# Attention and gated FFN on one core: the normalizing products move from VectorE to GpSimd, and the planned order is made anew

## The chip, the cores and the metric

The kernel runs on one core of a Trainium2 chip. The time is the device time of one execution in microseconds (us); lower is better. The profile shows one execution of the program, engine by engine: PE is TensorE (PEld its weight loads), DVE is VectorE, ACT is ScalarE, POOL is GpSimd, SP is SyncE, which here only issues DMA transfers.

## What is computed

```python
def reference(A_x, A_wqkv, A_wo, B_x, B_w_gate, B_w_up, B_w_down, gate_w):
    # x: 2048 x 512, 32 heads of width 16, F = 1376; all bfloat16
    x = A_x
    g = sigmoid((x * gate_w).sum(-1, keepdims=True))
    q, k, v = heads(x @ A_wqkv)
    p = softmax(q @ k.T * 16 ** -0.5)            # per head, 2048 x 2048
    a = merge_heads(p @ v) @ A_wo
    b = ((x @ B_w_gate) * (x @ B_w_up)) @ B_w_down
    return g * a + (1 - g) * b
```

The softmax is computed without a maximum: a column of ones beside each head's v makes the matmul with v also give the sum of the exponentials, and the attention output is divided by that sum afterwards. This division is the "normalizing product" of the title.

## The kernel before

**Tiling.** The queries come in 4 chunks of 512, the heads in 4 groups of 8. One chunk and one group are a *block* (16 of them, `bi` 0 to 15, about 40 us each); a block has two *quads* of 4 heads. For each quad and each of the 16 key tiles TensorE makes four score tiles of 128x512 in PSUM (tiles `QM` by `KT`; lines L1825 and L1803), the exponentials of them are made, and TensorE multiplies them with v (`Vp`, or the scaled copies `Vs`) into the output bank of the quad. TensorE works as eight tiles of 64x32 in two row halves.

**Two ways for the exponential.** For 10 of 16 key tiles ScalarE makes it (L1922; one to three score tiles at a time). For most of the other six (`dks`) VectorE makes a cheap 16-bit integer approximation in a buffer `DB` (L1962, the "pass"), and three copies of that buffer with a small integer added (steps v = 1, 2, 3) are multiplied with the scaled `Vs`, which refines the approximation. A copy is one 64-bit integer addition on GpSimd (`int64_add`, L1969, whole or in halves) or, more seldom, one instruction on VectorE (L1968). The buffers are the 8 of `DB` and, later on, the storage of `wv` and `wk`, which is why copies also read `DB<-wv`, `wk<-DB` and so on.

**Fillers.** Projections of q, k and v and the gated FFN run as filler matmuls between the attention work; VectorE evacuates them.

**The normalizing chain of a block.** VectorE copies the two output banks to `oc` and `oraw` (L2030); small transfers bring the sums together (`den8`); VectorE takes reciprocals (`recip`, L2044); they go out to DRAM (`scr_w`, tile `rscr`) and come back spread over the partitions (`rbc`, tile `rb`); and `mult` (L2133) makes `OT = oc * rb`, which later goes through the output projection. `oc` may be overwritten by the next block's copy only after `mult`. For the last block (15) half of the heads are normalized by another way at the very end (`tail_norm`, `tail_out`).

**Who sets the order.** `_Sched` is a planner that runs when the kernel is built: an event loop with a price for each kind of instruction decides for each engine what comes next, by rules and by tables in `PAR` with one value per microsecond of planned time. What comes out is one fixed list of instructions per engine, with semaphore waits between them. At run time each engine goes through its list in that order and stops at an instruction whose inputs are late. Relevant parts are `try_pool` (what GpSimd does next; `ptask` is a list of tasks for it, empty in this version; `small` holds VectorE's small tasks, the product among them), `issue` and `try_sp`: TensorE's instructions come in blocks of 256, the planner counts them (`icount`, `inext`), and the transfers whose price is in `BULK` are issued only in a window of time that is set from each block crossing (`land`), to keep them away from the fetch of the next block. Where the planner puts a `BULK` transfer in a window, the transfer also waits for a TensorE instruction.

**GpSimd's preparation.** The prologue runs a dummy `int64_add` on a tiny tile `lib` (L2179 and L2180) long before the first copy. Ahead of it the compiled program holds a pair of MODIFY_POOL_CONFIG instructions which the source does not name. A second such pair stands ahead of the one TENSOR_TENSOR that GpSimd executes in this version, an addition in `tail_out` (L2107) at the very end.

Of the kernel before, what the change touches and what calls it, by code (L numbers as in the profile page):

```python
# [12 lines left out]
ALU = mybir.AluOpType  # L13
# [123 lines left out]
class _Sched:  # L137
# [117 lines left out]
    def issue(self, r, n, key=None):  # L255
# [83 lines left out]
    def s_a(self, r):  # L339
        i = self.apos[r]  # L340
        p = None
        if self.apend[r] is None:
# [478 lines left out]
    def pe_phase(self, r):  # L821
        if self.ends():
            return self.pe_end(r)
        if self.g("lw") and self.lw[r]:
# [311 lines left out]
    def try_pool(self):  # L1136
# [5 lines left out]
        for x in self.ptask:  # L1142
            if x[0] <= now:
                self.ptask.remove(x)
                self.log("pool", x[1], x[3])
                self.pool_v = self.lock_v = self.now + x[1]
                self.at(self.pool_v)
                x[2]()
                return True
# [5 lines left out]
        for e in self.cpq:  # L1155
# [10 lines left out]
            else:  # L1166
                return False
            if not self.cp_buf(e, v):
                return False
# [9 lines left out]
            return True  # L1179
        return False  # L1180
# [7 lines left out]
    BULK = (2.0, 3.4, 4.0, 4.2)  # L1188

    def try_sp(self):  # L1190
# [3 lines left out]
        free = now > self.par["spend"] or self.land - 0.85 <= now + 1e-9 <= self.land + 0.05  # L1194
# [156 lines left out]
    def norm2(self, bi):  # L1351
# [21 lines left out]
    def norm3(self, bi, o):  # L1373
        c, b = divmod(bi, 4)
        op = self.hw.mult(bi, [o] + self.dep([("x", ch) for ch in range(1, min(self.par["xq"], 2) + 1)]) + self.rdep(("ocb", bi)) + self.rdep(("outl", c - 2))) if self.hw else None
# [260 lines left out]
    def run(self):  # L1636
# [54 lines left out]
        self.fullm, self.fullend = False, 0.0  # L1691
        self.lw, self.lk = [None, None], [None, None]
# [41 lines left out]
class _Hw:  # L1734
# [397 lines left out]
    def mult(self, bi, deps):  # L2132
        return self.dve(lambda v: v.tensor_tensor(self.OT[:, bi % 8, :], self.oc[:], self.rb[:], ALU.mult), deps)  # L2133
# [18 lines left out]
    def prologue(self):  # L2152
# [112 lines left out]
        for var in (0, 1):  # L2265
# [23 lines left out]
 'alook': ((7, 6), (1, 5), (2, 2), (1, 4), (3, 2), (1, 6), (15, 2), (1, 4), (43, 2), (1, 3), (12, 2), (1, 3), (2, 6), (1, 2), (2, 6), (2, 2), (1, 6),  # L2289
# [541 lines left out]
```

## Time and profile before

| | |
|---|---|
| time, median of 3 runs | 656.09 us (654.62 to 781.75) |
| the profiled execution's own time | 655.02 us |
| its span in the profile | 652.9 us |
| PE busy | 646.0 us, 99% |
| ACT busy | 638.9 us, 98% |
| DVE busy | 603.7 us, 92% |
| POOL busy | 523.3 us, 80% |
| granted TensorE clock | 1.00 |

The span leaves out 2.1 us of the profiled execution's time, which lie around it. Busy times count an engine as busy while an instruction of it runs; a busy PE is not necessarily one that has all eight tiles at work. Register, branch, semaphore and DMA-issuing instructions are not counted as busy.

### The profile page before, as it was taken

Reading aid. Unit: us, or ns where it says so; the run is one execution under the profiler, and the core shown is the slowest. Engines: PE = TensorE matmul, PEld = TensorE weight load, DVE = VectorE, ACT = ScalarE, POOL = GpSimd, SP = SyncE. Lnnn points to the kernel's source line nnn. Section 1 sums busy time; section 2 is a strip of 40 time slices with the busy share of each in tenths; the row PEclk is TensorE's granted clock in tenths of the full one; section 3 lists DMA queues with packets and bytes.
Section 4 is the critical chain, followed back from the end, with each engine's and each line's share of the span. In section 5 each row is a group of like instructions: output and inputs, shape, how many; then the busy total and the mean of one; then the engine's idle time right before and its main releaser. Section 6 shows DMA issues by size and latency. Waiting matters only on the chain.

```text
span 652.9 us, 46802 instructions
## 1 busy us (share of the span) xinstructions
PE 646.0 (99%) x22683; PEld 374.7 (57%) x20716; DVE 603.7 (92%) x996; ACT 638.9 (98%) x776; POOL 523.3 (80%) x602
## 2 busy tenths in 40 slices
PE   9999999999999999999999999999999999999997
PEld 4666556555555565555555655555555566665664
DVE  7899999999998989999999989999998899998995
ACT  6999999999999999999999999999999999999996
POOL 4229887898898999898999677899898756977871
PEclk9999999999999999999999999999999999999999
DMA  9201222221210100101001010100101011010101
GB/s 176 67 5 44 61 55 66 32 50 54 77 41 20 32 28 21 31 5 31 12 20 32 13 47 21 32 13 13 31 7 42 19 30 34 5 31 21 30 6 50
DMA packets 32498, 22.89 MB, mean 35 GB/s; under 512 B 17356, under 2 KB 29036, under 8 KB 32304
## 3 DMA queue, kind: packets, MB, share of 16 engines
q1 hardware_dynamic: 30784, 18.86, 11.5%
q8 instruction: 169, 2.77, 1.8%
q10 hardware_dynamic: 1488, 1.05, 0.7%
q14 instruction: 25, 0.20, 0.1%
q0 software_dynamic: 32, 0.00, 0.0%
HBM read 12.23 MB, written 2.36 MB: 22 GB/s over the span
## 4 chain that ended last, share of the span: by engine, by line
PE 95%; DVE 2%; POOL 1%; DMA 1%; ACT 1%; issue 0%; POOLq 0%; ACTq 0%; DVEq 0%
PE ps L1825 86%; PE ps L1803 9%; DVE DB L1962 1%; DMA wq<-in_A_wqkv_dram 1%; POOL DB L1969 0%; ACT wu L1922 0%; PE ps L2243 0%; POOLq L87 0%; PE ps L2075 0%; DVE hT L2004 0%; POOL wk L1969 0%; POOL wq L2062 0%; ACTq L2159 0%; ACT oc L2103 0%; DVE wk L1968 0%
## 5 line engine op out<-in xcount | busy, mean ns | idle before, releaser
L1825 PE MATMUL ps<-QM,KT 64*32 64x512 bf16 x6224 | 462.5, 378 | 0.3 <-issue 0.2
L1969 POOL INT64_ADD DB<-DB x385 | 341.1, 901 | 84.0 <-DVE DB L1962 29.1
L1962 DVE TENSOR_SCALAR DB<-ps 128x512 int16<-128x512 f32 x576 | 378.0, 689 | 25.3 <-PE ps L1825 21.2
L1922 ACT ACTIVATE PT<-ps 128x1024 bf16<-128x1024 f32 (+1 forms) x349 | 301.4, 949 | 1.5 <-PE ps L1803 0.6
L1825 PE MATMUL ps<-DB,Vs 64*17 64x512 bf16 x3368 | 300.8, 376 | 0.6 <-POOL DB L1969 0.4
L1922 ACT ACTIVATE xT<-ps 128x1024 bf16<-128x1024 f32 (+1 forms) x264 | 239.5, 987 | 0.7 <-PE ps L1825 0.6
L1825 PEld LDWEIGHTS ps<-QM,KT 64*32 64x32 bf16 x6224 | 140.4, 89 | 140.5 <-DVE DB L1962 32.1
L1803 PE MATMUL ps<-QM,KT 64*32 64x512 bf16 x1968 | 194.0, 376 | 0.1
L1825 PE MATMUL ps<-PT,Vp 64*17 64x512 bf16 x1222 | 170.4, 376 | 0.0
L1825 PE MATMUL ps<-xT,Vp 64*17 64x512 bf16 x960 | 143.6, 376 | 0.0
L1825 PE MATMUL ps<-DB,Vp 64*17 64x512 bf16 x1160 | 116.2, 376 | 0.0
L1825 PE MATMUL ps<-xT,wg 64*32 64x512 bf16 x1376 | 108.9, 376 | 0.0
L1825 PE MATMUL ps<-xT,wu 64*32 64x512 bf16 x1376 | 108.5, 377 | 0.0
L1825 PEld LDWEIGHTS ps<-DB,Vs 64*17 64x17 bf16 x3368 | 85.7, 86 | 28.3 <-PE ps L1825 3.8
L1825 PE MATMUL ps<-wd,hT 64*32 64x512 bf16 x1408 | 99.7, 376 | 0.0
L1922 ACT ACTIVATE wd<-ps 128x1024 bf16<-128x1024 f32 (+1 forms) x88 | 76.1, 955 | 0.5 <-PE ps L1803 0.2
L1969 POOL INT64_ADD wv<-DB x61 | 54.7, 901 | 3.0 <-DVE DB L1968 1.0
L1969 POOL INT64_ADD DB<-wk x51 | 43.6, 873 | 7.4 <-DVE wk L1962 4.9
L1825 PEld LDWEIGHTS ps<-PT,Vp 64*17 64x17 bf16 x1222 | 43.9, 86 | 9.9 <-PE ps L1825 2.3
L1825 PE MATMUL ps<-wv,Vs 64*17 64x512 bf16 x448 | 45.0, 376 | 0.0
L1825 PEld LDWEIGHTS ps<-xT,wg 64*32 64x32 bf16 x1376 | 36.8, 91 | 13.6 <-issue 2.3
L1969 POOL INT64_ADD DB<-wv x41 | 37.3, 924 | 8.9 <-DVE OT L2133 3.7
(126 smaller groups left out, 869.5 us busy)
## 6 DMA issues: line engine op xcount, KB each, us to landing
rb<-rscr SPq DMA_DIRECT2D x16, 256.0 KB
QM<-qraw SPq DMA_DIRECT2D x124, 16.0 KB, 2.3
oc<-oraw SPq DMA_DIRECT2D x60, 32.0 KB, 2.4
out_dram<-ost SPq DMA_DIRECT2D x12, 128.0 KB, 2.0
wd<-in_B_w_down_dram SPq DMA_DIRECT2D x10, 128.0 KB, 2.7
wu<-in_B_w_up_dram SPq DMA_DIRECT2D x12, 96.0 KB, 2.3
wg<-in_B_w_gate_dram SPq DMA_DIRECT2D x12, 96.0 KB, 2.6
OT<-in_A_x_dram SPq DMA_DIRECT2D x2, 256.0 KB, 3.5
```

Source lines behind the costliest of these rows:

```text
L1803: return pe.add_instruction(mybir.InstMatmult(name=self.nc.get_next_instruction_name(), engine=pe.engine, ins=[pe.lower_ap(rhs), pe.lower_ ...
L1825: o = pe.matmul(dst, lhs, rhs, start=st, stop=sp, tile_position=(64 * r, 32 * cc), skip_group_check=True)
L1922: return self.P.op("act", lambda a: a.activation(dst, src, ACT.Exp, scale=self.ES), deps)
L1962: return self.dve(lambda v: v.tensor_scalar(dst, src, self.YB, 0.0, ALU.add, ALU.max), deps)
L1969: return self.P.op("pool", lambda e: e.int64_add(o.bitcast(I64), a.bitcast(I64), 32 * v * 0x0001000100010001), deps)
```

## The change

Four things are changed in the planner, and one in the program it makes:

1. `mult` of blocks 0 to 14 becomes a GpSimd instruction; that of block 15 stays on VectorE. In the planner it becomes a `ptask` with a price of 1.29 us in place of a small VectorE task of 0.598 us. `try_pool` takes it when no copy can be started, or at once when it has been ready for `PLAG` = 6 us.
2. The window for `BULK` transfers moves: it ran from 0.87 to 1.77 us behind a block crossing and runs from 0 to 0.95 us behind it. The transfers of the reciprocals to DRAM (price 1.85) become `BULK`. A block is counted as 255.7 instructions.
3. The rule that takes PSUM banks in pairs for score tiles gets two more modes (`apair` 5 and 6), which may take a pair across the two row halves.
4. All 42 tables of `PAR` with values per microsecond have new values; no single-valued entry changes. So the order of the instructions is new on every engine.

```diff
-            self.inext += 256
+            self.inext += 255.7
             self.land = self.now + 1.72
...
-            self.at(self.land - 0.85)
...
-            if i % 2 == 0 and self.g("apair"):
-                p = self.pair_pick(self.g("apair") > 2) if self.nb["A"] + 2 <= self.g("amax") else None
-                if p is None and self.g("apair") in (2, 4):
+            if (i % 2 == 0 and self.g("apair")) or (self.g("apair") > 4 and self.apend[1 - r] is None):
+                p = self.pair_pick(2 < self.g("apair") < 5) if self.nb["A"] + 2 <= self.g("amax") else None
+                if p is None and self.g("apair") in (2, 4, 6):
                     return False
...
-            bank, self.apend[r] = self.take_pair("A", p)
+            o = 1 - r if self.g("apair") > 4 and self.apend[1 - r] is None else r
+            self.across[o] = o != r
+            bank, self.apend[o] = self.take_pair("A", p)
...
 def try_pool(self):
-        for x in self.ptask:
-            if x[0] <= now:
-                ...
-                return True
+        if self.pool_task(now - self.PLAG):
+            return True
...
-                return False
+                return self.pool_task(now)
...
+    PLAG = 6.0
+
+    def pool_task(self, now):
+        for x in self.ptask:
+            if x[0] <= now:
+                self.ptask.remove(x)
+                self.log("pool", x[1], x[3])
+                self.pool_v = self.lock_v = self.now + x[1]
+                self.at(self.pool_v)
+                x[2]()
+                return True
         return False
...
-    BULK = (2.0, 3.4, 4.0, 4.2)
+    BULK = (1.85, 2.0, 3.4, 4.0, 4.2)
...
-        free = now > self.par["spend"] or self.land - 0.85 <= now + 1e-9 <= self.land + 0.05
+        free = now > self.par["spend"] or self.land - 1.72 <= now + 1e-9 <= self.land - 0.77
...
-                    self.small.append((t2 + self.par["mmarg"], 0.598, lambda: self.norm3(bi, o2), ("M", bi)))
+                    if bi < 15:
+                        self.ptask.append((t2 + self.par["mmarg"], 1.29, lambda: self.norm3(bi, o2), ("M", bi)))
+                        self.at(t2 + self.par["mmarg"] + self.PLAG)
+                    else:
+                        self.small.append((t2 + self.par["mmarg"], 0.598, lambda: self.norm3(bi, o2), ("M", bi)))
...
     def mult(self, bi, deps):
-        return self.dve(lambda v: v.tensor_tensor(self.OT[:, bi % 8, :], self.oc[:], self.rb[:], ALU.mult), deps)
+        return self.P.op("pool" if bi < 15 else "dve", lambda v: v.tensor_tensor(self.OT[:, bi % 8, :], self.oc[:], self.rb[:], ALU.mult), deps)
...
  PAR = {
- 'alook': ((7, 6), (1, 5), (2, 2), (1, 4), (3, 2), (1, 6), (15, 2), (1, 4), (43, 2), ...
+ 'alook': ((8, 6), (5, 2), (2, 5), (67, 2), (1, 3), (5, 2), (1, 6), (12, 2), (1, 6), ...
```

How the lists move is shown at three places. The rows are the compiled lists of one engine, in order: line, operation, output tile and input tiles, shape, how often in a row, and the semaphores waited for (`s_pe0`, `s_pe1`, `s_dve`, `s_pool`: those engines; `s_drb`, `s_docb`, `s_dscr`: the transfers into `rb`, into `oc` and to `rscr`). A row ISA with two tiles is a copy; a bare row ISA is a pair of MODIFY_POOL_CONFIG. Lines of the changed kernel are 20 to 30 higher.

GpSimd before, the copies that it made while VectorE made the first product (at 78 us):

```order
L1969 ISA DB<-DB 128x1024 [waits s_pe1]
L1969 ISA wv<-DB 128x1024 [waits s_pe0]
L1969 ISA DB<-DB 128x1024 [waits s_pool,s_dve]
L1969 ISA DB<-DB 128x1024 [waits s_dve,s_pe0]
L1969 ISA DB<-DB 128x1024 [waits s_pool]
L1969 ISA DB<-DB 128x1024 [waits s_pe1]
```

GpSimd after, around the first product:

```order
L1993 ISA DB<-DB 128x1024 [waits s_pool,s_dve]
L1993 ISA wv<-DB 128x1024 [waits s_pe0]
L1993 ISA DB<-DB 128x1024 [waits s_pe1]
L2157 ISA
L2157 TENSOR_TENSOR OT<-oc,rb 128x512 [waits s_drb,s_docb]
L1993 ISA
L1993 ISA DB<-DB 128x1024 [waits s_dve,s_pe0]
L1993 ISA DB<-DB 128x1024 [waits s_pe1]
L1993 ISA DB<-DB 128x512 [waits s_pe0]
L1993 ISA DB<-DB 128x512
```

Between two copies there now stand a bare ISA, the product, and another bare ISA. The same three rows stand at each of the 15 products: the list of GpSimd has 3 bare ISA before and 33 after.

VectorE before, around the first product and the copy of the next block's output into `oc`:

```order
L1962 TENSOR_SCALAR DB<-ps 128x512 [waits s_pe0]
L1968 TENSOR_SCALAR DB<-DB 128x2048
L2133 TENSOR_TENSOR OT<-oc,rb 128x512 [waits s_drb,s_docb]
L1962 TENSOR_SCALAR DB<-ps 128x512 [waits s_pe1]
L2030 TENSOR_TENSOR oc<-ps,erow 128x512 [waits s_dve,s_pe0]
L2004 TENSOR_TENSOR hT<-ps,usb 128x512 [waits s_pe1]
```

VectorE after, around the same copy:

```order
L1986 TENSOR_SCALAR DB<-ps 128x512 [waits s_pe0] x2
L1986 TENSOR_SCALAR DB<-ps 128x512 [waits s_pe1]
L1986 TENSOR_SCALAR DB<-ps 128x512 [waits s_pe0]
L2054 TENSOR_TENSOR oc<-ps,erow 128x512 [waits s_pool]
L1986 TENSOR_SCALAR DB<-ps 128x512 [waits s_pe1]
L2028 TENSOR_TENSOR hT<-ps,usb 128x512 [waits s_pe0]
```

The product is gone from VectorE's list, and the copy into `oc` waits for GpSimd instead.

SyncE before, the transfers of the second block's reciprocals:

```order
L2040 DMA oc<-oraw 16x512 x3
L2130 DMA rscr<-rec 4x16x32 [waits s_dve]
L2130 DMA rscr<-rec 4x16x32
L2056 DMA wg<-in_B_w_gate_dram 128x384 [waits s_pe0]
L2125 DMA rb<-rscr 128x1x512 [waits s_dscr,s_pe1]
```

SyncE after:

```order
L2064 DMA oc<-oraw 16x512 x3
L2080 DMA wu<-in_B_w_up_dram 128x384 [waits s_pe0]
L2154 DMA rscr<-rec 4x16x32 [waits s_pe0] x2
L2149 DMA rb<-rscr 128x1x512 [waits s_dscr,s_pe0]
L2080 DMA wu<-in_B_w_up_dram 128x384 [waits s_pe1]
```

The transfers to `rscr` now wait for TensorE too, that is for a window behind a block crossing.

The amount of work stays as it is: 22687 matmuls before and 22679 after, 1352 score tiles exponentiated by ScalarE in 763 instructions before and 767 after, 696 score tiles passed by VectorE in both, 369 transfers and other rows of SyncE in both. GpSimd's copies are 394 whole ones and 194 halves before, 379 and 227 after.

More of the change, by code (lines that the diff above doesn't have):

```diff
@@ L823, in pe_phase @@
             return self.pe_end(r)
+        if self.across[r]:
+            if self.apend[r] is None:
+                self.across[r] = False
+            elif self.s_a(r):
+                return True
         if self.g("lw") and self.lw[r]:
@@ L1141, in try_pool @@
         now = self.now + 1e-9
-        for x in self.ptask:
-            if x[0] <= now:
[L1144 to L1148, printed above, removed]
-                return True
+        if self.pool_task(now - self.PLAG):
+            return True
         if self.dve4_until + 0.063 > now:
@@ L1166, in try_pool @@
             else:
-                return False
+                return self.pool_task(now)
             if not self.cp_buf(e, v):
-                return False
+                return self.pool_task(now)
             for k in hs:
@@ L1179, in try_pool @@
             return True
+        return self.pool_task(now)
+    PLAG = 6.0
[7 more added lines that the diff above has]
+                x[2]()
+                return True
         return False
@@ L1374, in norm3 @@
         c, b = divmod(bi, 4)
-        op = self.hw.mult(bi, [o] + self.dep([("x", ch) for ch in range(1, min(self.par["xq"], 2) + 1)]) + self.rdep(("ocb", bi)) + self.rdep(("outl", c - 2))) if self.hw else None
+        op = None
+        if self.hw:
+            deps = [o] + self.dep([("x", ch) for ch in range(1, min(self.par["xq"], 2) + 1)]) + self.rdep(("ocb", bi)) + self.rdep(("outl", c - 2))
+            op = self.hw.mult(bi, deps + ([self.last4] if bi < 15 else []))
+        if bi < 15:
+            self.setr(("ot", bi), self.now + 1.29 + 0.044 + 0.05, op)
+            return
         self.last4 = op
@@ L1691, in run @@
         self.fullm, self.fullend = False, 0.0
+        self.across = [False, False]
         self.lw, self.lk = [None, None], [None, None]
@@ new lines @@
+ 'anyb': 0,
+ 'apair': ((7, 0), (1, 3), (4, 2), (1, 1), (2, 0), (1, 1), (3, 0), (1, 3), (7, 0), (1, 4), (2, 0), (1, 1), (4, 0), (2, 1), (1, 3), (3, 1), (1, 0),
[15 rows of a table added]
+ 'apick': ((8, 0), (35, 1), (5, 0), (2, 1), (2, 0), (4, 1), (13, 0), (2, 1), (3, 0), (1, 1), (1, 0), (6, 1), (1, 0), (5, 1), (1, 0), (12, 1), (1, 0),
[8 rows of a table added]
+ 'ares': ((12, 2), (1, 1), (2, 2), (1, 1), (5, 2), (10, 1), (4, 2), (2, 1), (1, 2), (4, 1), (4, 2), (2, 3), (2, 2), (2, 3), (1, 1), (3, 2), (8, 3),
[10 rows of a table added]
+ 'await': ((7, 0.6), (1, 0.05), (3, 0.6), (1, 0.05), (4, 0.1), (5, 0.05), (2, 0.1), (1, 0), (4, 0.1), (1, 0.05), (1, 0.22), (1, 0.45), (4, 0),
[17 rows of a table added]
@@ new lines @@
+ 'cpmax': ((8, 20), (5, 5), (3, 20), (5, 5), (4, 8), (1, 3), (5, 8), (4, 10), (8, 8), (3, 30), (1, 14), (1, 5), (2, 10), (2, 14), (1, 10), (11, 14),
[13 rows of a table added]
+ 'dact': ((26, 2), (1, 5), (25, 2), (1, 5), (15, 2), (3, 5), (2, 2), (9, 5), (1, 2), (3, 5), (2, 3), (1, 2), (3, 3), (5, 5), (1, 2), (2, 4), (1, 5),
[11 rows of a table added]
+ 'dahead': ((8, 0), (5, 1), (3, 2), (5, 1), (4, 0), (1, 1), (3, 0), (1, 1), (3, 0), (2, 1), (11, 0), (2, 1), (2, 0), (2, 1), (4, 2), (3, 1), (6, 0),
[9 rows of a table added]
+ 'dend': ((7, 2), (1, 4), (7, 2), (1, 0), (15, 2), (1, 0), (3, 5), (8, 2), (3, 0), (2, 1), (1, 0), (1, 4), (2, 1), (1, 2), (16, 1), (2, 4), (3, 1),
[11 rows of a table added]
@@ new lines @@
+ 'dresv': ((16, 1), (4, 0), (1, 1), (1, 0), (1, 1), (5, 0), (2, 1), (1, 0), (4, 1), (13, 0), (2, 1), (1, 0), (1, 1), (12, 0), (1, 1), (37, 0), (3, 1),
[7 rows of a table added]
+ 'dwait': ((6, 0), (1, 0.1), (1, 0.4), (3, 0), (1, 0.6), (1, 0.2), (3, 0), (5, 0.6), (7, 0), (1, 0.6), (1, 0.4), (1, 0.1), (4, 0.6), (11, 0.1),
[16 rows of a table added]
+ 'fcf': ((22, 1), (1, 0), (7, 1), (1, 0), (15, 1), (2, 0), (2, 1), (2, 0), (1, 1), (33, 0), (2, 1), (1, 0), (3, 1), (2, 0), (3, 1), (6, 0), (2, 1),
+        (20, 0), (1, 1), (1, 0), (1, 1), (83, 0), (2, 1), (9, 0), (2, 1), (73, 0), (1, 1), (51, 0), (4, 1), (48, 0), (1, 1), (4, 0), (2, 1),
+        (93, 0), (4, 1), (1, 0), (2, 1), (4, 0), (2, 1), (34, 0), (1, 1), (8, 0), (2, 1), (2, 0), (1, 1), (4, 0), (1, 1), (17, 0), (1, 1), (10, 0),
+        (1, 1), (50, 0)),
@@ new lines @@
+ 'flim': ((42, 99), (1, 0), (80, 99), (3, 8), (2, 99), (1, 4), (34, 99), (1, 2), (1, 0), (2, 99), (4, 2), (19, 99), (5, 4), (20, 99), (1, 8),
[4 rows of a table added]
+ 'fmax': ((6, 3), (1, 1), (12, 3), (1, 2), (2, 3), (1, 2), (23, 3), (2, 2), (1, 1), (1, 3), (2, 2), (1, 3), (20, 2), (1, 1), (14, 2), (1, 3), (3, 2),
[9 rows of a table added]
+ 'fres': ((8, 1), (79, 0), (1, 1), (45, 0), (1, 1), (11, 0), (1, 1), (5, 0), (1, 1), (62, 0), (1, 1), (1, 0), (1, 1), (14, 0), (8, 1), (3, 0),
[10 rows of a table added]
+ 'fstart': ((21, 2), (25, 1), (2, 2), (2, 1), (2, 2), (1, 1), (39, 2), (6, 1), (4, 2), (3, 1), (1, 2), (6, 1), (16, 2), (1, 1), (11, 2), (2, 1),
[6 rows of a table added]
@@ L2648 @@
+ 'ghalf': ((13, 0.1), (2, 0.5), (1, 0.7), (1, 0.1), (3, 0.5), (1, 0.1), (8, -1), (1, 0.3), (1, -1), (4, 0.7), (8, -1), (3, 0.7), (2, 0.3), (1, 0.5),
[15 rows of a table added]
+ 'gwin': ((15, 0.2), (1, 0), (5, 0.2), (6, 0.8), (1, 1.2), (1, 0.8), (1, 0.2), (8, 0.8), (4, 0.2), (4, 0.8), (2, 1.2), (2, 0.8), (2, 0.5), (1, 0.8),
[15 rows of a table added]
  'ift': 3.55,
```

54 lines of the change are left out of this document (16 added, 38 removed), and 852 rows, old and new, of the table PAR.

## The prediction

> **What bounds the kernel now.** I read the busy times first, then the chain that ended last, then what PE waited for:
>
> ```profile
> span 652.9 us, 46802 instructions
> PE 646.0 (99%) x22683; PEld 374.7 (57%) x20716; DVE 603.7 (92%) x996; ACT 638.9 (98%) x776; POOL 523.3 (80%) x602
> ...
> PE 95%; DVE 2%; POOL 1%; DMA 1%; ACT 1%; issue 0%; POOLq 0%; ACTq 0%; DVEq 0%
> ...
> PE ps L1825 <- POOL DB L1969: 0.4, 1, 0.4
> ```
>
> PE runs 646.0 of 652.9 us, ACT 638.9, and 95% of the chain is PE. The longest wait of a matmul for a copy of POOL was 0.4 us. So the planned order fits the machine almost without a gap, and there is next to no idle time on PE or ACT from which a new delay could be paid: a delay that reaches PE goes into the total. Since the amount of matmuls, exponentials and passes stays the same (22687 and 22679 matmuls, 1352 score tiles for ACT, 696 for DVE), the change can win at most what PE now stands idle, 6.9 us, part of it at the start and the end. What it can lose has no such limit.
>
> POOL, which gets the new work, is the engine with the most room, but that room is in small pieces:
>
> ```profile
> core 0: us, PE busy (x) PEld busy (x) DVE busy (x) ACT busy (x) POOL busy (x), PEclk, DMA share, GB/s
> 0.00:24.00 24.00, 22.60 (x528) 13.00 (x472) 19.30 (x48) 18.28 (x32) 8.50 (x16) 1.00 0.81 164
> ...
> 200.00:300.00 100.00, 99.82 (x3564) 55.63 (x3232) 92.63 (x148) 99.30 (x125) 94.10 (x112) 1.00 0.08 22
> ```
>
> ```profile
> L1969 POOL INT64_ADD DB<-DB x385: 603/1037/1060, 13.8 to 636.6; - x193
> ...
>   DVE DB L1962: 30.8, 27
>   PE ps L1825: 28.1, 21
>   DVE DB L1968: 19.1, 9
>   PE ps L1803: 9.3, 7
> ...
>   PEld ps L1825: 3.1, 9
> ```
>
> A whole copy takes 1.04 us, a half 0.61. Ahead of copies POOL was idle for 87.3 us in these 64 waits, 1.4 us each on average. The last row is the other side: weight loads waited for copies 9 times, 3.1 us in all, so copies come just in time. How early they come is seen where a tile can be told apart by its name, at the first copies into `wv` and into `wk` and the first matmuls that read them:
>
> ```profile
> 50.65 1.04 POOL L1969 INT64_ADD wv<-DB  x1
> ...
> 53.83 0.39 PE L1825 MATMUL ps<-wv,Vs 64*17 64x512 bf16 x4
> ...
> 129.80 1.04 POOL L1969 INT64_ADD wk<-DB  x1
> ...
> 133.36 0.39 PE L1825 MATMUL ps<-wk,Vs 64*17 64x512 bf16 x4
> ```
>
> The copies ended at 51.7 and 130.8 and were read 2.1 and 2.5 us later: a **lead** of 2.3 us.
>
> **The change: the products on POOL.** On DVE a product is an ordinary instruction, and 15 of the 16 leave it:
>
> ```profile
> L2133 DVE TENSOR_TENSOR OT<-oc,rb x16: 679/682/686, 78.2 to 640.3; 128x512 bf16<-128x512 f32 x16
> ```
>
> That takes 15 x 0.68 = 10.2 us of busy time off DVE. DVE has 49 us of idle time and the chain runs 2% through it, so I count this as nothing; DVE will wait for score tiles 10 us longer.
>
> On POOL a product does not come alone: in the compiled list there is a bare ISA row ahead of it and another behind it, each the pair MODIFY_POOL_CONFIG. The list of before has this pair where POOL goes over to `int64_add` and where it goes back to TENSOR_TENSOR at the end. The profile shows both:
>
> ```profile
> L2180 POOLq MODIFY_POOL_CONFIG  x2: 11/11/11, 1.0 to 1.1; - x2
> ...
> 7.86 0.18 POOL L2180 INT64_ADD lib<-lib  x1 [7.03 <-issue]
> ...
> L2107 POOLq MODIFY_POOL_CONFIG  x2: 18/18/18, 637.2 to 637.3; - x2
> ...
> 648.27 0.69 ACT L2103 ACTIVATE oc<-ps,gq 128x512 f32<-128x512 f32 x1 [0.48 <-PE ps L2098]
> ...
> 649.14 1.26 POOL L2107 TENSOR_TENSOR hT<-oc,wu 128x512 bf16<-128x512 f32 x1 [11.92 <-ACT oc L2103]
> ```
>
> The pair itself takes 11 to 18 ns. But the first `int64_add` behind it, on a tile of 128x4, started only at 7.86, **6.8 us** behind the pair at 1.1; the profile names no other engine for the idle 7.03 us, only "issue", and the instruction itself took 0.18. I read this as the price of going over: POOL does nothing until the code of the other kind is in place. The way back, to TENSOR_TENSOR, is hidden: its pair ran at 637.3, and the product of the tail had to wait for ACT until 648.96 anyway; it started 0.18 us after that. So the way back costs between nothing and 11.7 us and runs from the pair on, not from the first use. I take it to cost the same as the way there, the only row of its kind.
>
> The Trainium skill, page "GPSIMD Engine Reference", section "2.1 Instruction dispatch", states that the first call to a freshly loaded kernel of that engine pays about 6 us (5.95 measured), without an instruction of its own in the profile. The trace of before agrees in kind and has 6.8. By the page's 5.95 alone, in place of the value that I take next, the time below would be 797 us, an estimate.
>
> The one row was taken in a stretch in which transfers kept the DMA engines busy (share 0.81 until 24 us, 0.08 later). If the switch fetches something, it may be quicker later; no row says how much. I take **6.3 us**, half a us off the row, and keep nothing and 6.8 as ends.
>
> The sum for one product: POOL stands between two copies for 6.3 (there) + 1.26 (the product, as in the row at 649.14) + 6.3 (back) = 13.9 us. The planner counts 1.29 us and puts it where no copy can be started, which is a gap of 1.4 us. Of the rest, 12.5 us, the next copies' lead of 2.3 us hides a part. Behind that PE, in its fixed list, stands at the first matmul that reads a late copy, for **10.2 us**. Queued behind it are score matmuls, so ACT and DVE run dry; nothing overtakes. Between products (some 40 us) POOL can win back 2.3 us of lead from its small gaps, so each product pays anew. 15 x 10.2 = **153 us**; 652.9 + 153 = 806 us of span, and with the 2.1 us by which the execution's time of 655.02 exceeds its span, **808 us**. The median of the runs, 656.09, is 1 us above that execution, which is nothing beside it.
>
> A check from POOL's side: 13.8 us until its first copy, 379 x 1.04 + 227 x 0.61 = 533 us of copies, 15 x 13.9 = 209 us, and 16 us from its last copy (637.2) to the end make 772 us if it never waited again. So with two open switches the span can't be near 653, and 806 leaves POOL 34 us of its old waiting.
>
> **A second wait on the same product.** The copy of the next block's output into `oc` waits for the product. On DVE before:
>
> ```profile
> 100.28 0.68 DVE L2030 TENSOR_TENSOR oraw<-ps,erow 128x512 f32<-128x512 f32 x1
> ...
> 104.55 0.34 DVE L2044 RECIPROCAL rec<-den 128x32 f32<-128x32 f32 x1
> ...
> 113.52 0.68 DVE L2133 TENSOR_TENSOR OT<-oc,rb 128x512 bf16<-128x512 f32 x1
> ...
> 120.64 0.68 DVE L2030 TENSOR_TENSOR oc<-ps,erow 128x512 f32<-128x512 f32 x1
> ```
>
> Product to next copy is 7.1 us here. After, the product can stand up to 6 us in the planner's list and ends 6.3 + 1.26 us behind the last copy of POOL, so DVE will sometimes stand at the copy into `oc` with all its passes behind it, for some us. POOL is standing in the same us and for longer (its second switch comes after the product), so I add nothing; if the two don't overlap, the price is inside the upper end.
>
> **The transfers and the block crossings.** SP's list moves: the transfers to `rscr` now wait for PE, behind a crossing. Crossings come every 652.9/169 = 3.9 us:
>
> ```profile
> q8 instruction: 169, 2.77, 1.8%
> ```
>
> That puts up to 3.9 us, 2 on average, into the normalizing chain, from reciprocal to product 9.0 us in the rows above. It delays only the product; the planner knows of it, and 7.1 us of distance to the next `oc` cover it. Without that cover it would be up to 15 x 2 = 30 us, in the same waits as above. For the crossings themselves the gain is bounded by PE's idle time: 6.9 us or less, and nothing below that reason. I take nothing. **The bank pairs and the new tables** give the same work in another order: within 6.9 us to the good; to the bad an order that is as dense as the old would cost nothing, and one that lets PE wait as now and once more is again 7 us. Nothing, with 7 us to both sides.
>
> **The rivals.** *One open switch* (713 us): the way back to TENSOR_TENSOR is cheap or has time to run while the product waits for its transfers. Then 6.3 + 1.26 - 1.4 - 2.3 = 3.9 us for each product, 58 us, 711 of span. For it: the hidden pair at 637.3 has no lower bound. Against it: the pair stands directly behind a copy, and the planner starts the product 0.6 us after its input is due.
>
> *No slack* (above 860): the copies behind a product have less lead than the two shown (the 9 late weight loads), or DVE's wait for `oc` adds up. Without the lead it is 15 x (6.8 + 1.26 + 6.8 - 1.4) = 202 us, 857 us; without anything hidden 15 x 14.9 = 223, 878 us.
>
> *No switch* (652 us), the rival on the other side: the 6.8 us are paid once, when the code comes for the first time, and a later pair finds it in place, in a few tenths of a us. The place is the same idle time behind each pair; it decides from (1.4 + 2.3 - 1.26)/2 = 1.2 us per switch downwards: below that the gap and the lead hide both. Then the products are free, DVE has 10.2 us more room, and what is left is the order, 655 within 7 us; half of PE's idle time won would be 652. For it: the trace shows each kind's switch only once, so no repeated one. Against it: the pair stands in the list each time and is of one form.
>
> The Trainium skill, same page, section "4.1 Engine selection", advises against elementwise work with two inputs on this engine, as about twice as slow as VectorE. The trace has 1264 against 682 ns, a ratio of 1.85. By that rule alone the products would cost 15 x 0.58 = 9 us of POOL's time, which its gaps hide; the time would be that of this last rival.
>
> **How the numbers follow.** Two open switches 0.66, one 0.15, no slack 0.05, no switch 0.14. The forecast is the likeliest, 808 us. The range has to take in one switch and most of the unknown prices: 700 (one switch, with 0.9 us more hidden at each product) to 860 (two at 6.8 without the lead), which leaves out the no-switch case and the worst. A measurement of this kernel can tell about 2% (13 us) from no change. Of the no-switch case's 0.14 I put 0.03 below 643 us and 0.11 within 2%; all others are slower, 0.86.
>
> **What the profile after would show.** If I am right: POOL idle for some 6 us ahead of each TENSOR_TENSOR `OT<-oc,rb` and ahead of the first copy behind it, with no engine named for it ("issue"); POOL's busy time near 550 us and its idle time 200 us more; in the waits of PE about 15 long ones for POOL's copies, 8 to 12 us each; PE, ACT and DVE with nearly unchanged busy times in a longer span; POOL on the chain in 15 places. A single idle stretch of 6 us at each product is the one-switch rival. If the copies run on within a us of the product, no switch is paid, and then the forecast is wrong at its first step. It would also be wrong if the stretches are there but PE's waits are much shorter than 10 us: then the lead is larger than the two rows say.

## The result, and the profile after

| | before | after |
|---|---|---|
| time, median of the runs | 655.74 us | 863.79 us (862.2 to 868.18) |
| ratio to before | | 1.318, 95% interval 1.314 to 1.323 |
| profiled execution: its time / span | 655.02 / 652.9 us | 862.2 / 860.4 us |
| mean granted clock of TensorE | 1.0 | 0.891 |

One of the four runs of before took 781.75 us, in a slower state, and the ratio leaves it out. The change costs 208 us, about 13.9 us for each product. The forecast was 808 us with a range up to 860: the kernel became slower and GpSimd stands at each product, as forecast, but the loss is over a third larger than the 153 us of the sum, and the time lies 4 us above the range. The page of the profile after, busy times and chain:

```profile
span 860.4 us, 46950 instructions
PE 689.8 (80%) x22675; PEld 375.9 (44%) x20756; DVE 599.1 (70%) x982; ACT 643.6 (75%) x780; POOL 546.7 (64%) x635
...
PE 71%; issue 16%; DVE 8%; POOL 5%; ACT 0%; POOLq 0%; DVEq 0%
```

Two things are to be seen. PE no longer fills the span: 860.4 - 689.8 = 170.6 us are idle, where 6.9 were. And its busy time itself rose by 43.8 us, although it does nearly the same matmuls (22679 for 22687). The chain has 16% "issue", which no engine is named for. The waits say where that stands (engine, tile and line that waited, what released it; us in total, times, longest):

```profile
PE ps L1849 <- POOL DB L1993: 110.1, 15, 12.8
...
POOL OT L2157 <- issue: 98.5, 14, 7.7
...
POOL DB L1993 <- issue: 83.0, 17, 6.2
...
DVE oc L2054 <- POOL OT L2157: 65.5, 11, 6.7
...
PE ps L1849 <- DVE oc L2054: 33.7, 6, 6.5
...
PE ps L1849 <- POOL OT L2157: 12.8, 2, 6.5
```

POOL stands at the products (L2157) and again at the copies behind them (L1993), with "issue" as the only name. PE's longest waits are now for POOL's copies, 15 of them, where the longest had been 0.4 us. One product seen whole, POOL's rows of the timeline (start, duration, line, operation; idle time ahead in brackets):

```profile
84.90 1.06 POOL L1993 INT64_ADD DB<-DB  x1
92.77 1.25 POOL L2157 TENSOR_TENSOR OT<-oc,rb 128x512 bf16<-128x512 f32 x1 [6.82 <-issue]
99.98 4.40 POOL L1993 INT64_ADD DB<-DB  x6 [5.95 <-issue]
```

6.8 us of standing ahead of the product, 1.25 us of product, 6.0 us behind it: 14.0 us between two copies. Over the 15 products these pieces average 7.0, 1.25 and 5.9 us, 14.15 us with 13.6 and 15.2 as extremes. In the same stretch, PE's rows:

```profile
88.62 0.39 PE L1827 MATMUL ps<-QM,KT 64*32 64x512 bf16 x4
94.81 0.61 PE L1849 MATMUL ps<-xT,wq 64*32 64x512 bf16 x4 [5.80 <-DVE oc L2054]
...
101.06 0.60 PE L1849 MATMUL ps<-DB,Vs 64*17 64x512 bf16 x4 [5.22 <-POOL DB L1993]
...
102.33 0.64 PE L1827 MATMUL ps<-QM,KT 64*32 64x512 bf16 x4
```

PE stands twice: first for the copy into `oc`, which waits for the product, then for the first late copy. And the matmuls behind the first stall take 0.60 to 0.64 us in place of 0.39. The stretches of the profile show why (from:to, length, busy time of PE, PEld, DVE, ACT, POOL; then the granted clock):

```profile
75.00:85.00 10.00, 9.91 (x312) 4.58 (x268) 10.00 (x16) 9.92 (x13) 10.00 (x11) 1.00 0.20 52
...
95.00:100.00 5.00, 0.85 (x12) 0.00 (x0) 0.95 (x2) 0.00 (x0) 0.02 (x1) 0.50 0.01 2
...
102.00:104.00 2.00, 2.00 (x48) 0.88 (x36) 1.23 (x2) 1.08 (x2) 2.00 (x5) 0.50 0.00 0
...
106.00:108.00 2.00, 2.00 (x88) 1.12 (x72) 0.35 (x1) 1.96 (x3) 2.00 (x4) 1.00 0.21 57
```

The clock granted to TensorE fell to 0.50 in the stall and stayed there for some 4 us of full work behind the second stall. Over the run the stretches at 0.50, idle time included, add up to 190 us in the trace's clock record.

### The profile page after: what moved, and what is told of

It is laid out like the page before. It is cut to its first block, busy times and chain, and to the rows that moved or that the text cites. A ratio compares the mean times of both kernels' runs of the same rounds, so it can differ in the third digit from the quotient of the medians.

```text
span 860.4 us, 46950 instructions
## 1 busy us (share of the span) xinstructions
PE 689.8 (80%) x22675; PEld 375.9 (44%) x20756; DVE 599.1 (70%) x982; ACT 643.6 (75%) x780; POOL 546.7 (64%) x635
## 4 chain that ended last, share of the span: by engine, by line
PE 71%; issue 16%; DVE 8%; POOL 5%; ACT 0%; POOLq 0%; DVEq 0%
PE ps L1849 64%; PE ps L1827 6%; DVE DB L1986 5%; POOL DB L1993 2%; POOL OT L2157 2%; DVE oc L2054 1%; DVE wv L1986 1%; PE ps L2240 0%; DVE wk L1986 0%; DVE usb L2024 0%; DVE xT L2017 0%; DVE hT L2028 0%; PE ps L2249 0%; DVE qraw L2008 0%; PE ps L2099 0%
## 5 line engine op out<-in xcount | busy, mean ns | idle before, releaser
L1849 PE MATMUL ps<-QM,KT 64*32 64x512 bf16 x6272 | 475.1, 392 | 28.4 <-DVE oc L2054 27.9
L1986 DVE TENSOR_SCALAR DB<-ps 128x512 int16<-128x512 f32 (+1 forms) x572 | 376.4, 689 | 108.1 <-PE ps L1849 104.7
L1993 POOL INT64_ADD DB<-DB x397 | 343.0, 878 | 166.7 <-issue 83.0
L1849 PE MATMUL ps<-DB,Vs 64*17 64x512 bf16 x3376 | 309.1, 391 | 110.4 <-POOL DB L1993 110.1
L1827 PE MATMUL ps<-QM,KT 64*32 64x512 bf16 x1920 | 193.4, 394 | 6.0 <-DVE oc L2054 5.8
L1849 PE MATMUL ps<-PT,Vp 64*17 64x512 bf16 x1198 | 185.1, 395 | 0.0
L1849 PE MATMUL ps<-xT,Vp 64*17 64x512 bf16 x982 | 153.9, 392 | 0.0
L1849 PE MATMUL ps<-wd,hT 64*32 64x512 bf16 x1408 | 103.3, 401 | 12.8 <-POOL OT L2157 12.8
L1946 ACT ACTIVATE wd<-ps 128x1024 bf16<-128x1024 f32 (+1 forms) x97 | 76.6, 886 | 14.8 <-PE ps L1849 13.3
L2157 POOL TENSOR_TENSOR OT<-oc,rb 128x512 bf16<-128x512 f32 x15 | 18.8, 1252 | 105.4 <-issue 98.5
L1986 DVE TENSOR_SCALAR wv<-ps 128x512 int16<-128x512 f32 x64 | 42.3, 686 | 27.4 <-PE ps L1849 27.0
L2054 DVE TENSOR_TENSOR oc<-ps,erow 128x512 f32<-128x512 f32 x14 | 9.7, 691 | 73.2 <-POOL OT L2157 65.5
L1993 POOL INT64_ADD wv<-DB x57 | 51.3, 904 | 3.9 <-DVE DB L1992 2.0
L1993 POOL INT64_ADD DB<-wv x54 | 44.9, 849 | 8.4 <-PE ps L1827 4.2
L1849 PEld LDWEIGHTS ps<-wd,hT 64*32 64x32 bf16 x1408 | 36.9, 97 | 29.6 <-issue 20.4
```

The lines of the kernel that those rows point to most:

```text
L1827: return pe.add_instruction(mybir.InstMatmult(name=self.nc.get_next_instruction_name(), engine=pe.engine, ins=[pe.lower_ap(rhs), pe.lower_ ...
L1849: o = pe.matmul(dst, lhs, rhs, start=st, stop=sp, tile_position=(64 * r, 32 * cc), skip_group_check=True)
L1946: return self.P.op("act", lambda a: a.activation(dst, src, ACT.Exp, scale=self.ES), deps)
L1986: return self.dve(lambda v: v.tensor_scalar(dst, src, self.YB, 0.0, ALU.add, ALU.max), deps)
L1993: return self.P.op("pool", lambda e: e.int64_add(o.bitcast(I64), a.bitcast(I64), 32 * v * 0x0001000100010001), deps)
L2054: return self.dve(lambda v: v.tensor_tensor(dst, self.ps[:, ob, :], self.erow[:], ALU.mult), deps)
```

## The experiments

All ratios are to the kernel before on the same chip. To put kernels of different chips side by side, a ratio is multiplied by 655.7 us.

**What the new order is worth.** First the changed list with the products back on DVE:

```
-        return self.P.op("pool" if bi < 15 else "dve", lambda v: v.tensor_tensor(...), deps)
+        return self.dve(lambda v: v.tensor_tensor(...), deps)
```

> The changed kernel with its list word for word, except that the 15 products are issued to DVE again, at the same places in the list. No code of POOL has to be switched. Theory A (the 207 us are the price of switching POOL's code twice for each product): 650 to 665 us; what differs from the 655.7 us of before is the value of the new order alone, and DVE's products, which the planner did not reserve room for there, may cost up to 10 us. Theory B (the new order, its crossings and bank pairs, is a good part of the loss): above 680 us. TensorE's busy time is 646 us by A, since without the stalls its clock stays at 1.0.

Measured: ratio 1.020 (1.014 to 1.027), 13 us. Theory A asked for at most 9 us over before and theory B for 24 or more, so neither range fits, but 13 of 208 us is not "a good part". DVE does here what the planner had no room for on it, so a second kernel takes the products off DVE too, and leaves POOL busy for about the planned time without a switch:

```
+        if bi < 15:
+            for k in range(2):
+                o = self.P.op("pool", lambda g: g.memset(self.OT[:, bi % 8, :], 0.0), deps if k == 0 else [o])
+            return o
```

> The changed kernel with each of the 15 products replaced by two fills of the same 128x512 block of OT with zero, on POOL, at the same place and with the same waits; what leaves the kernel out is the product itself, so the attention output is missing from the result. It has all of the change but the switch: DVE is relieved of its 10.2 us, POOL is busy at the planned place, and the copy into oc waits as planned. Theory A: within 10 us of before, 645 to 665 us, and better than e1_order (DVE's unplanned products cost e1_order part of its 15 us). Theory B' (the new order itself is worse than the old by those 15 us): about 670 us, like e1_order.

Measured: 1.012 (1.007 to 1.017), 8 us; its page:

```profile
span 667.4 us, 46900 instructions
PE 656.1 (98%) x22675; PEld 375.1 (56%) x20756; DVE 597.4 (90%) x982; ACT 643.3 (96%) x780; POOL 542.0 (81%) x650
...
PE 96%; DVE 2%; issue 1%; DMA 0%; ACT 0%; POOLq 0%; DVEq 0%
```

e9_fill leaves out the product itself, and with it the switch. So even without the switch, and with DVE relieved of its 10 us, the changed list is not faster than the old one; by the ratio it is 8 us slower, which is less than the 2% that count as a difference here. PE is 98% busy again at full clock. The two ratios overlap, so what the unplanned products cost DVE is not settled.

**The switch alone, the time alone.** Both stand on e1_order. One adds a tiny product on tiles of its own, the other fills as long as a product:

```
+            self.P.op("pool", lambda v: v.tensor_tensor(self.ty[:], self.tx[:, 0:4], self.tx[:, 4:8], ALU.mult), [])
```
```
+            for k in range(5):
+                self.txo = self.P.op("pool", lambda g: g.memset(self.tx[:], 0.0), [getattr(self, "txo", None)])
```

> As e1_order, with one TENSOR_TENSOR of 128x4 elements on POOL at each of the 15 places, on tiles of its own: nothing waits for it and it waits for nothing but its turn in POOL's list. It takes the switch by itself, without the product's time and without its waits. Theory A: both switches are still paid, 13 us of POOL at each place in place of 14.15, so e1_order plus 15 x 12 to 13 = 180 to 200 us, some 835 to 860 us. Rival C (what stalls is the chain through the product, its late inputs and the copy into oc that waits for it): nothing waits for this small instruction, so less than e1_order plus 30 us. Rival D (one open switch): e1_order plus some 60 us.

> As e1_order, with five fills of 128x224 on POOL at each of the 15 places, about as long together as a product (1.25 us), on a tile of its own; the fill is an operation for which before's trace shows no switch. Theory A: POOL's 1.4 us of gaps and the lead of its copies hide the time: e1_order plus 0 to 10 us, and no idle stretch of 6 us on POOL. Rival E (the time of an elementwise instruction on POOL is itself the loss, since the copies behind it have no lead): e1_order plus 15 us or more.

Measured: e2_switch 1.285 (1.277 to 1.294), e3_time 1.015 (1.008 to 1.022). The time of a product on POOL costs nothing that can be seen; an instruction of 0.19 us with a switch on both sides costs (1.285 - 1.020) x 655.7 = 174 us, 11.6 for each, a little under the 180 to 200 of theory A. POOL's timeline of e2_switch, and a row of its waits:

```profile
93.29 0.19 POOL L2160 TENSOR_TENSOR ty<-tx 128x4 bf16<-128x4 f32 x1 [7.25 <-issue]
99.36 4.40 POOL L1995 INT64_ADD DB<-DB  x6 [5.88 <-issue]
```

```profile
PE ps L1851 <- POOL DB L1995: 146.9, 15, 11.6
```

The same two stands as in the changed kernel, with nothing that waits for the small instruction itself. Rivals C and D fall.

**Half of the products, and the old order.** e4_half leaves the products of even blocks to DVE; e6_before_pool is the kernel before with the engine of the 15 products changed and nothing else:

```
+        return self.P.op("pool" if bi < 15 and bi % 2 else "dve", ...)
```

> The changed kernel with only the 7 products of odd blocks on POOL; the 8 of even blocks up to the fourteenth go to DVE, at their places. Theory A, each product paying for itself: e1_order plus 7/15 of the difference between the changed kernel and e1_order, about 750 us if e1_order is 655. If lateness adds up from product to product, since copies cannot win back their lead within 40 us, fewer products cost less than their share: below 735 us. If a switch is dearer after a longer pause, more: above 765 us.

> The kernel before with the one edit of the engine: the 15 products on POOL, at the places where DVE had them, nothing else of the change. Theory A (two switches for each product): the planner of before gave POOL no room there, so at least as dear as the changed kernel's 13 us for each: 655 + 195 = 850 us or more, up to 880. Rival H (the changed kernel's places are what makes the switches dear, since they stand right ahead of copies that are due): clearly less, below 820 us.

Measured: e4_half 1.152 (1.142 to 1.163), which is 755 us at 655.7: (1.152 - 1.020) x 655.7 / 7 = 12.3 us for a product, against (1.318 - 1.020) x 655.7 / 15 = 13.0 with all 15. Each pays for itself; there is no once-only price. e6_before_pool 1.316 (1.310 to 1.323), the changed kernel's ratio. Its waits, PE for the copies and POOL for its own code:

```profile
PE ps L1825 <- POOL DB L1969: 112.3, 14, 12.4
...
POOL OT L2133 <- issue: 97.8, 14, 7.7
```

So the places that the new planner chose were no cheaper than the old ones: with the switch the new order as a whole is neither better nor worse than the old. Rival H falls.

**The clock.** The question was how much of the loss is slow matmuls. e5_warm gives PE matmuls with zero weights to do while it stands (`WARM` counts groups of four):

```
+    WARM = {"A": 20, "B": 30}
...
+                            o = pe.matmul(dst, self.zz[lo:hi, 0:17], x, start=False, stop=True, ...)
```

> The changed kernel with matmuls whose weights are zero, added into an output bank that is open anyway (they add nothing): 80 of them ahead of the matmul that waits for the copy into oc, 120 ahead of the first matmul that waits for a copy behind a product, 14 and 15 places. They wait for nothing new, so that TensorE has work in most of each stall. Everything else stands where it stood. Theory F (TensorE's granted clock falls to 0.5 after an idle stretch, and the matmuls behind it run slow for some us; that is the 44 us by which its busy time rose): most of the 44 us come back, though the stalls stay: 820 to 840 us, with a mean granted clock near 1.0 in place of 0.89. Rival G (the busy time rose for another reason, such as matmuls that wait inside the array): the added matmuls win nothing and cost what they overlap: 860 us or more.

Measured: 1.448 (1.434 to 1.461), far slower; its runs lie between 941 and 973 us. This was a fault of the experiment: the added matmuls were longer than the stalls, and many of them ran at half clock. It decides nothing on F and G, but showed something else (last section). The second try gives each stall its own length (here `WARM` has, for each group of PE's list that stalled, the us to fill; the loop makes groups of four matmuls):

```
+    WARM = {671: 5.8, 674: 5.22, 1008: 6.3, 1017: 4.13, 1339: 6.47, ...}
...
+        for i in range(int(us / (0.182 if len(banks) > 1 else 0.2213))):
```

> A second try for the clock. In e5_warm the added matmuls took longer than the stalls (16 us against 11 for each product, and at half clock far more), so it could not tell the theories apart. Here each of the 24 stalls that the trace of the changed kernel shows gets added matmuls with zero weights for just its length (3.6 to 12.8 us, at 0.055 us for one at full clock), ahead of the matmul that stalled. Theory F (idle time drops the granted clock, and the slow matmuls behind it are 31 to 44 us of the loss): the clock stays near 1.0 and the time falls to 820 to 840 us. Rival G (the rise of TensorE's busy time is not the clock's): 855 us or more. If the clock falls although TensorE has these matmuls to do, it is not idle time alone that drops it, and the time stays or grows.

Measured: 1.293 (1.286 to 1.301), mean clock 0.985: less than theory F asked for, though the clock was back. One place had 560 added matmuls where 228 were meant, and the clock still fell behind 7 of the stalls. e12_warm3 mends the first and fits the lengths to the stalls that e10_warm2 showed; e11_again is the changed kernel beside it:

> The changed kernel once more, unaltered, beside e12_warm3 on the same chip, so that the clock's share is a difference on one chip: 1.31 to 1.325 of before.

> As e10_warm2, with the added matmuls fitted to the stalls that e10_warm2 itself showed (up to 1.8 us longer; one place where twice too many stood is mended), so that next to no idle time is left in a stall. In e10_warm2 the mean granted clock came back from 0.89 to 0.985 and TensorE's own matmuls from 690 to 661 us, but by the ratios to before the time fell by only 17 us, since TensorE reached the next stall earlier and stood there longer. Theory F' (that is so: the slow clock costs 17 us net, since the ends of the stalls hang on POOL): 15 to 22 us less than e11_again, clock 0.99 or above. Theory F (the slow clock costs its full 31 to 44 us, and e10_warm2 lost the rest to its own faults): 30 us or more less than e11_again.

Measured: e11_again 862.95 us, 1.316 (1.311 to 1.320); e12_warm3 841.11 us, 1.282 (1.278 to 1.286), clock 0.996. The difference is 22 us, the upper end of theory F'. In the page and the groups of e12_warm3 the added matmuls take the place of the idle time:

```profile
PE 825.0 (98%) x25828; PEld 447.2 (53%) x23912; DVE 599.4 (71%) x982; ACT 643.3 (77%) x780; POOL 546.3 (65%) x636
...
L1869 PE MATMUL ps<-KT,zz 64*17 64x512 bf16 x3152 | 174.5, 376 | 0.0
```

PE's own work is 825.0 - 174.5 = 650.5 us, 39 us less than in the changed kernel, and the stalls are 174.5 + (838.3 - 825.0) = 188 us, 17 us more than its 170.6. So of 39 us of slow matmuls 22 are lost, and the rest only takes the place of waiting: the stalls end when POOL is done, and a faster PE reaches them sooner. Another reading of the 17 us would be that the added matmuls ran on after POOL was done. The trace excludes it: at 20 of the 24 places the matmul that had stalled started 0.05 to 0.07 us behind the end of what it waited for, at the other four 0.15 to 0.46 us.

**What POOL's standing hides.** The last question was the size of the stand that the gap and the lead swallow, and whether a switch costs more than its time. Three kernels take e9_fill and put more fills ahead of and behind those that stand in a product's place, without any switch (6, 12 and 20 on each side; the trace of each shows two MODIFY_POOL_CONFIG pairs, like that of before, where the changed kernel's shows 32):

```
+            for k in range(6):
+                o = self.P.op("pool", lambda g: g.memset(self.tx[:], 0.0), (deps if k == 0 else []) + [o])
```

> No switch at all: e9_fill (fills in place of the 15 products, so the attention output is missing here too) with 6 more fills of 128x224 ahead of each and 6 behind it, 0.33 us each with their gaps as e3_time showed them. POOL stands between two copies for about 5.0 us of work in place of the 14.15 us of the changed kernel. It measures the term that the prediction took as 3.7 us hidden for each product (gap 1.4 and lead 2.3). Theory P (3.7 us hidden): e9_fill plus 15 x 1.3 = 20 us. Theory Q (about 2 us hidden, as 12.0 us of loss from 14.15 us of stand with the clock kept up in e12_warm3 say): plus 15 x 3.0 = 45 us.

> The same with 12 fills ahead and 12 behind, 9.0 us of stand at each of the 15 places (attention output missing). Theory P: e9_fill plus 15 x 5.3 = 80 us. Theory Q: plus 15 x 7.0 = 105 us, and up to 20 us more where the clock falls after the stalls.

> The same with 20 fills ahead and 20 behind, 14.3 us of stand, as long as two switches and a product (attention output missing). Theory A says that a switch costs only the time for which POOL stands, so this kernel, without any switch, loses what the changed kernel loses: e9_fill plus 190 to 205 us, a ratio to before near 1.31. Theory P: plus 159 us and the clock's share of about 20, near 1.285. If it is clearly below 1.28, the switch costs more than its time.

The stand is the mean time between two copies of POOL around these places, from their rows in each trace; the loss is the ratio less that of e9_fill, times 655.7 / 15:

| kernel | stand at each place | ratio (95%) | loss for each |
|---|---|---|---|
| e9_fill | 1.3 us | 1.012 (1.007 to 1.017) | 0 |
| e13_stand5 | 5.2 us | 1.090 (1.088 to 1.093) | 3.4 us |
| e14_stand9 | 9.3 us | 1.207 (1.202 to 1.211) | 8.5 us |
| the changed kernel | 14.15 us | 1.318 (1.314 to 1.323) | 13.4 us |
| e15_stand14 | 14.8 us | 1.328 (1.324 to 1.332) | 13.8 us |
| e12_warm3, clock kept up | 14.2 us | 1.282 (1.278 to 1.286) | 11.8 us |

Over e9_fill the three kernels lose 51, 128 and 207 us. Theory P asked for 20, 80 and some 180, theory Q for 45 and 105 to 125, theory A for 190 to 205: Q and A come nearest, each a few us short.

The changed kernel lies on the line of the fills: between e14_stand9 and e15_stand14, 14.15 us of stand would lose 13.2 us. A switch costs the time for which POOL stands, and nothing that these runs could see beyond it. PE's waits of e15_stand14, without a switch, are those of the changed kernel:

```profile
PE ps L1850 <- POOL DB L1994: 122.4, 15, 12.7
```

With the clock kept up, 14.2 us of stand lose 11.8: **2.4 us** are hidden, give or take 0.3 by the intervals. In e13_stand5 5.2 - 3.4 = 1.8 are hidden, and at most some 1.0 more if its 31 us at half clock are taken off the loss. Theory Q, not P.

How much of the 2.4 is gap and how much lead can be bounded by the trace of e9_fill. At 11 of the 15 places the next copy follows the fills at once (within 0.02 us), so there the gap is no longer than the stand of 1.03 to 1.07 us; at the other four the whole stand is gap. That makes a gap of 0.6 to 1.3 us on average, and leaves 1.1 to 1.8 us for the lead, an estimate.

**Two lists that say little.** e7_window is the kernel before with the transfers' window (the line below, the crossing every 255.7 and the list of bulk prices) and nothing else; e8_planned_dve is the changed kernel with the products planned and issued on DVE:

```
-        free = now > self.par["spend"] or self.land - 0.85 <= now + 1e-9 <= self.land + 0.05
+        free = now > self.par["spend"] or self.land - 1.72 <= now + 1e-9 <= self.land - 0.77
```

> The kernel before with only the crossing's part of the change: the crossing every 255.7 rather than 256 counted instructions, transfers issued in a window behind the crossing rather than ahead of it, and the shorter bulk price in that list. Products stay on DVE, the tables are those of before, and the planner makes the order anew from them. If the window has an effect of its own, it shows here: the prediction put it at nothing, within 7 us. The tables were not made for it, so an order that is up to 2% worse says nothing of the window.

> The changed kernel with its tables, window and bank pairs, but the 15 products planned and issued on DVE as before. Against e1_order, which has them on DVE without room in the plan, it tells whether e1_order's 15 us over before are the unplanned products (then 655 to 665 us here) or the order that the new tables make (then 670 us or more).

Measured: 1.086 (1.083 to 1.090) and 1.109 (1.105 to 1.112). The first line is of the page of e7_window, the second of e8_planned_dve:

```profile
PE 698.3 (98%) x22524; PEld 360.4 (51%) x20660; DVE 618.5 (87%) x1010; ACT 662.5 (93%) x944; POOL 448.9 (63%) x505
```

```profile
PE 709.5 (98%) x22308; PEld 363.1 (50%) x20472; DVE 606.5 (84%) x984; ACT 679.8 (94%) x936; POOL 411.2 (57%) x487
```

ACT has 944 and 936 instructions in place of 776: the planner, with tables made for other rules, cut many exponentials in two (488 and 447 of them work on a single score tile, where before has 175) and moved copies from POOL to DVE. Each is a different program, so they tell nothing of the window or of the planned products, and e8_planned_dve does not settle what e1_order left open: whether the window has an effect of its own stays open. That the old tables are to blame for the 8.6% and 10.9% is likely, but not shown.

## What of the prediction was right, and the steps that failed

*The bound.* "A delay that reaches PE goes into the total" held: PE's idle time rose by 164 us of the 208 by which the span grew. The other 44 are PE's own busy time, for which the sum had no term.

*The switch.* Right, in both directions and every time: 7.0 us on average ahead of the products, 5.9 behind, together 12.9 against the predicted 12.6. That the sum came so close is in part luck. The row at 7.86 is a switch to `int64_add`, 6.8 us from its pair; the later switches of that kind, behind the products, take 5.4 to 6.0 us from theirs, so half a us off was the right way and not enough. Whether the first is longer for the busy transfers, or for being the first, was not tried. The switch to TENSOR_TENSOR, for which before gave no more than 11.7 us as an upper bound, takes 6.7 to 7.6 us from its pairs, more than the 6.3 assumed. The two errors cancel. The Trainium skill, page "GPSIMD Engine Reference", section "2.1 Instruction dispatch", gives about 6 us for the first call to a freshly loaded kernel of the engine. The traces agree in size, 7.0 and 5.9 us, and show that here it is paid at every change of kind: 30 times in one run.

*The rivals.* "One open switch" and "no switch" fall by the two stands at each product and by e2_switch. The worst case, "no slack", named 857 us, close to the result, but for a wrong reason: it takes nothing but the gap of 1.4 us off a stand of 14.9, where the runs show 2.4 us taken off 14.15 and 1.5 us added by the clock. Its number was right by chance.

*The products' own time, DVE's relief, the second wait.* Counted as nothing, and the runs don't contradict it. e3_time shows it of the products' time. In e9_fill no gain from DVE's relief is seen, but the new order's own cost, of about the same size, can't be told apart from it. The second wait is seen (DVE stands at `oc` for 65.5 us, and PE behind it for 33.7), but it ends before POOL's own standing does; e2_switch, whose stand is 0.9 us shorter, loses nearly as much for each place without it (11.6 us, against 13.0 over e1_order).

*The steps that failed* stand in the sum for one product, at two terms: what gap and lead hide was put too high, and the slow clock behind a stall was left out. A smaller term stands beside them:

| term | predicted | measured | 15 products |
|---|---|---|---|
| POOL stands between two copies | 13.9 us | 14.15 us | +4 us |
| hidden by gap and lead | 3.7 us | 2.4 us | +20 us |
| slow clock behind the stalls | none | 1.5 us (22 us / 15) | +22 us |
| the new order itself | 0, within 7 us | 8 us in all | +8 us |

Together +54 us on the predicted 153, 207 of the measured 208. That they add up is no test of them, since the hidden part and the clock are differences of the same ratios. The last row is the least sure: 8 us are less than the 2% that count as a difference, and e6_before_pool loses as much with the old order.

The clock is the term that was missing. "PE, ACT and DVE with nearly unchanged busy times" was the sign that failed, for PE alone. The trace of before could not show it, since PE never stood long enough there. The Trainium skill has the rule, page "TensorE: Matmul & The Clock Gate", section "What's actually happening": an idle window of about 3.4 us puts the clock to half, and about 3.4 us of work bring it back. The traces agree on the fall, 0.50 behind stalls such as the 5.80 us above, and roughly on the return, with some 4 us of full work there. The prediction forecast 15 stalls of 10 us on PE and did not ask what they do to the clock. Counting every slow matmul in full would have added too much: of the 39 us by which PE's work grew only 22 reach the end.

The 3.7 us were a gap of 1.4 and a lead of 2.3. The gap was the mean of the 64 waits ahead of copies that were quoted, though most of the 588 copies of before started without a wait; at the products' places it is at most 1.3 us by e9_fill. The lead was taken from two copies, the first into `wv` and `wk`, and by the estimate above it is 1.1 to 1.8 us at the products. The 9 late weight loads, quoted as a sign against the lead, pointed the right way.

*What was to be seen.* POOL's busy time (546.7 for "near 550") and its idle time (313.7 us, 184 more, for "200 more") came as forecast. PE's long waits came as 24 pieces of 3.6 to 12.8 us rather than 15 of 8 to 12, because a wait for `oc`, or for the product itself, cuts nine of them in two.

## What to carry to other kernels

Look in GpSimd's compiled list for MODIFY_POOL_CONFIG. Here each pair of them, between `int64_add` and TENSOR_TENSOR in either direction, made the engine stand for 5.4 to 7.6 us, every time, so that an instruction of 0.19 us cost 11.6; fills between the copies had no such pair and no such stand. Other kinds of code were not tried. What such a stand costs in the end is its length less the lead of the work behind it; put fills of known length at the place to measure that lead, and do not read it off the easiest rows. And where a forecast has the busiest engine stand for some us, ask what clock it gets behind the stall, but count only what of the slow stretch does not fall into the next wait.

## What the runs showed of the hardware that was not expected

**Some matmuls hold the clock, but do not bring it back.** In e5_warm the added matmuls use 64 of the rows at a time and come at some 18 per us, against 31 of the kernel's own (312 in 75.00:85.00 of the changed kernel); their weights are zero. Two stretches of its profiled run of 973 us, filled mostly by them:

```profile
323.00:326.00 3.00, 3.00 (x68) 1.36 (x59) 0.00 (x0) 1.30 (x2) 1.27 (x1) 1.00 0.07 19
326.00:330.00 4.00, 3.93 (x84) 1.64 (x80) 1.98 (x3) 0.00 (x0) 0.00 (x0) 1.00 0.01 2
330.00:334.00 4.00, 4.00 (x91) 1.81 (x80) 0.00 (x0) 0.00 (x0) 2.35 (x3) 1.00 0.01 4
```

```profile
502.00:508.00 6.00, 6.00 (x68) 1.90 (x60) 0.01 (x1) 0.00 (x0) 3.06 (x3) 0.50 0.00 0
508.00:514.00 6.00, 6.00 (x60) 2.04 (x56) 2.48 (x4) 0.00 (x0) 1.20 (x2) 0.50 0.01 3
514.00:520.00 6.00, 6.00 (x64) 2.04 (x60) 0.00 (x0) 0.00 (x0) 0.00 (x0) 0.50 0.00 0
```

In the first, entered at full clock, the clock stayed at 1.00 for 11 us of them. In the second, entered at 0.50, it stayed at 0.50 for 18 us and more, though PE is busy throughout; it came back only behind them, with the kernel's own matmuls. The same run shows this at 11 places, 8.7 to 22.4 us of added matmuls each, at which the clock was at 0.50 and stayed there to their end. That is longer than the about 3.4 us of work that the Trainium skill, page "TensorE: Matmul & The Clock Gate", section "What's actually happening", names, so PE being busy by the profile is not what the clock goes by alone. What it does go by, the rows in use, the rate or the zero weights, was not tried.

**Short stalls are enough beside such matmuls.** In e10_warm2 the clock still fell to 0.50, for 3.4 us each time, behind 7 stalls that the added matmuls had filled but for 0.9 to 1.9 us; behind four other gaps of 0.9 to 1.4 us it did not. The Trainium skill, page "TensorE: Matmul & The Clock Gate", section "HAM oscillation — how this bites in real kernels", gives as the rule that PE should have no idle gaps above about 3.4 us; here shorter ones were enough when the work around them was of this thin kind.
